# A short convolution before a feed-forward layer: the first convolution in four 64x64 array tiles, a larger first load of w_in, and one x load moved

## The chip, the cores and the metric

The kernel runs on one core of a Trainium2 chip. A core has TensorE (PE in the profile) for matrix products, VectorE (DVE), ScalarE (ACT) and GpSimd (POOL) for elementwise work, SyncE (SP) for issuing transfers, and 16 DMA engines that all queues share. The metric is device time in microseconds. "Before" is the median of five runs.

## The reference

x has 8 batches of 4096 tokens with 192 channels. Eight heads of 24 channels each have seven taps. The taps of a head go through a softmax, and each head convolves its channels causally along the tokens. The result goes through a feed-forward layer with 2048 hidden units and ELU between its two products:

```
w = softmax(weight, axis=-1)                       # 8 heads x 7 taps
att[b, s, h, :] = sum_k w[h, k] * x_pad[b, s + k, h, :]   # six zero rows ahead of s = 0
h = att.reshape(32768, 192) @ w_in                 # 192 x 2048
g = where(h > 0, h, exp(min(h, 0)) - 1)
out = g @ w_out                                    # 2048 x 192
```

The kernel takes and gives FP32, and computes its products in BF16 and FP16 with FP32 accumulation.

## The kernel before

**Tiling.** The 32768 tokens form 32 supergroups of 1024. A supergroup has two groups of 512 tokens, group 0 and 1. Channels are split in three chunks j = 0, 1, 2 of 64 (eight of each head's 24 channels), and chunk data of group 0 lies in partitions 0 to 63, of group 1 in 64 to 127, so one 128-partition tile holds a chunk of both groups. The hidden units are split in 16 blocks q of 128. A step n is one q of one supergroup: for each group r, three H matmuls (L1006, one per chunk, 64 rows by 128 columns of the array, 512 tokens) fill one PSUM bank. One such bank is called a unit here.

**The ELU chain.** Each unit passes ScalarE's exp (L752, H to E), GpSimd's clamp to at most one (L705, on E in place) and VectorE's last step (L868: max(E - 1, H), written to gT in FP16), which also frees the bank. Then the output matmuls (L1029) multiply gT with w_out. The units pass the three engines in one order, each engine in its own program order.

**Order on TensorE.** A planner writes TensorE's order out when the program is built. It has two clocks, one for each group (and row half of the array), and puts H matmuls (h), convolution matmuls (c) and output matmuls (o) where its clocks and its model of the ELU chain say that they can run. The first 16 steps are planned with the function live, the rest by emit. PSUM has eight banks, and a bank that is to be reused waits for its reader. Engines run their lists in order, so an instruction whose wait is open holds everything behind it.

**Start.** Only supergroup 0 is convolved by another path than the rest. x for it arrives in xs. ScalarE casts it to BF16, chunk by chunk (L727, xb). TensorE transposes it (L929) in 64x64 tiles on the array's diagonal, chunk 3 meaning the eight halo rows (L940). VectorE evacuates chunk 0 and the halo (L824) and ScalarE chunks 1 and 2 (L739) to xT, with channels in partitions and tokens along the row. The convolution (L957) is then seven matmuls per chunk, one for each tap, whose 128x128 weights, taps, are diagonal matrices; chunks 0 and 1 leave two taps each to VectorE (L833, L838), which adds them while evacuating (L851). Chunk 2 has all taps on TensorE, in two half rows in two banks, evacuated by ScalarE (L743) and VectorE (L853). The results are att, the input of the first 16 steps. The other supergroups are convolved from xg with a band matrix Tm (L981), which is built in DRAM from wband (VectorE, L816) by two transfers that SyncE issues (L1052, L1061).

**Loads.** GpSimd issues w_in in two sets of three loads (L642: columns of q 0 to 3, then of q 4 to 15), then w_out (L653, three loads) and x of supergroups 1, 2 and 3 (L622, two loads each), and goes to its clamps after that. Later x loads stand between the clamps, at the unit that x_before names. w_in is loaded to partitions 0 to 63; the second copy in partitions 64 to 127, for group 1, is made by ScalarE for q 0 to 3 (L733) ahead of the convolution's last evacuation, by VectorE for q 4 to 7 (L856) after it, by ScalarE for q 8 after the seventh exp, and by a transfer of SyncE (L1069) for q 9 to 15.

The constants that set this:

```
WCOLS = ((0, 4 * FC), (4 * FC, 16 * FC))
UPPER = ((0, 4 * FC), (4 * FC, 8 * FC), (8 * FC, 16 * FC))
X3_AT = (0, 0)
ON_DVE = (2, 2, 0)
```

Of the kernel before, what the change touches and what calls it, by code (L numbers as in the profile page):

```python
# [39 lines left out]
WARM = (6, 1, 4)  # L40
WCOLS = ((0, 4 * FC), (4 * FC, 16 * FC))
UPPER = ((0, 4 * FC), (4 * FC, 8 * FC), (8 * FC, 16 * FC))
WOUT = (0, 4, 8, 16)
X3_AT = (0, 0)
HALO = 8
BW = P
ON_DVE = (2, 2, 0)
XL = GS - CW * (NWIN - 1) + PAD
# [18 lines left out]
ZERO_AT = 8  # L67
TAIL = 18


def bass_lightweight_conv__then__act_elu_kernel(
# [247 lines left out]

    start_up = [("t", j) for j in (0, 3, 1, 2)] + [("d", j) for j in range(3)]  # L320
    for i, (b, what) in enumerate(
# [6 lines left out]
    for rt in range(2):  # L328
        for g in range(2):
            turns[rt][g] += [(0, q, q + 1, 2 * q + rt) for q in range(LIVE - EARLY_O[g])]  # L330
    live(LIVE, [(n, m) for n in range(LIVE) for m in conv_steps.get(n, ())], turns)
    for n in range(LIVE, NP):
# [79 lines left out]
    with ExitStack() as stack:  # L412
# [34 lines left out]
        wcol = sbuf("wcol", [P, KSIZE], FP32)  # L447
        part = sbuf("part", [P, 2, GS], FP32)
        xl = sbuf("xl", [XL, D], FP32)
# [23 lines left out]
        s_xt = sema("s_xt")  # L473
        s_first = sema("s_first")
        s_fa = sema("s_fa")
# [48 lines left out]
        def att_need(s):  # L524
# [8 lines left out]
            ("d", 0): (0, 3),  # L533
            ("d", 1): (0, 4),
            ("d", 2): (3, 5),
        }
# [6 lines left out]
        def transposed(j):  # L543
            if j == 3:
                return xT[:, :, 0:HALO], H[:, bank_of["t", 3], 0 : 3 * HALO].rearrange(
                    "p (j c) -> p j c", j=3
                )
            return xT[:, j, HALO : HALO + GS], H[:, bank_of["t", j], :]

        def first_att(j, c0, c1):  # L550
# [164 lines left out]
        def _scalar(a):  # L715
# [9 lines left out]
            W(s_xs, 16)  # L725
            for j in range(3):
                a.activation(  # L727
                    xb[:, j, :, :].rearrange("p i (h e) -> p (i h) e", e=8),
                    xs[:, :, :].rearrange("p i (h j e) -> p j (i h) e", j=3, e=8)[:, j],
                    ACT.Copy,  # L730
                ).then_inc(s_cast)
            def upper_half(c0, c1):
# [4 lines left out]
            for j in range(1, 3):  # L737
                W(s_xt, j + 2)
                a.activation(*transposed(j), ACT.Copy).then_inc(s_fa)  # L739
            W(s_w[0], 48)  # L740
            upper_half(*UPPER[0])
            W(s_first, 3)
            a.activation(*first_att(2, 0, GS // 2), ACT.Copy).then_inc(s_fa)  # L743
            for item in act_order:
                if item[0] == "c":
                    m = item[1]
                    W(s_cv, m + 1 - CU)
                    a.activation(*conv_evac(W, m), ACT.Copy).then_inc(s_ce)  # L748
                elif item[0] == "h":
                    i = unit_at[item[1:]]  # L750
                    W(s_h, i + 1)
                    a.activation(  # L752
                        E[:, i % NE, :], H[:, bank_of[item], :], ACT.Exp
                    ).then_inc(s_exp)
                    if i == COPY_AT:
                        W(s_w[1], 48)
                        upper_half(UPPER[2][0], FC * LATE_Q)
                else:
                    a.activation(*out_evac(W, *item[1:]), ACT.Copy).then_inc(s_oev[item[2]])  # L759
# [4 lines left out]
        def _vector(v):  # L764
# [3 lines left out]
            v.memset(wband[:], 0.0).then_inc(s_wb)  # L768
            v.memset(xbh[:, :, 0, :], 0.0).then_inc(s_xz)
            W(s_wb, 1)  # L770
# [37 lines left out]
                ALU.mult,  # L808
            ).then_inc(s_tap)
            W(s_xh, 16)  # L810
            W(s_xz, 1)
            v.tensor_copy(
                xbh[:, :, 1, :].rearrange("p j (h e) -> p j h e", e=8),
                xh[:, :].rearrange("p (h j e) -> p j h e", j=3, e=8),
            ).then_inc(s_xz)
            v.tensor_copy(  # L816
# [4 lines left out]
            ).then_inc(s_tap)  # L821
            for at, j in enumerate((0, 3)):
                W(s_xt, at + 1)
                v.tensor_copy(*transposed(j)).then_inc(s_fd)  # L824
            W(s_fd, 2)
            for i in range(ON_DVE[0]):
                for j in range(2):
                    tap = KSIZE - 1 - i
                    src = xT[:, j, HALO - PAD + tap : HALO - PAD + tap + GS]
                    w = wcol[:, tap : tap + 1]  # L830
                    if i == 0:
                        W(s_fa, j)
                        ins = v.tensor_scalar(  # L833
                            out=part[:, j, :], in0=src, scalar1=w, scalar2=None, op0=ALU.mult
                        )
                    else:
                        W(s_part, 2 * i + j - 1)
                        ins = v.scalar_tensor_tensor(  # L838
                            out=part[:, j, :],
                            in0=src,  # L840
                            scalar=w,
                            in1=part[:, j, :],
                            op0=ALU.mult,
                            op1=ALU.add,
                        )
                    ins.then_inc(s_part)
            for j in range(2):
                W(s_part, 2 * ON_DVE[j] - 1 + j)
                W(s_first, j + 1)
                to, at = first_att(j, 0, GS)  # L850
                v.tensor_tensor(to, at, part[:, j, :], ALU.add).then_inc(s_fd)  # L851
            W(s_first, 3)
            v.tensor_copy(*first_att(2, GS // 2, GS)).then_inc(s_fd)  # L853
            c0, c1 = UPPER[1]
            W(s_w[1], 48)
            v.tensor_copy(w_in[HP:P, :, c0:c1], w_in[0:HP, :, c0:c1]).then_inc(s_wc)  # L856
            for item in dve_order:
# [20 lines left out]
        def _tensor(pe):  # L878
            W = Waits(pe)

            def wait_bank(what):
# [9 lines left out]
                else:  # L891
                    evacuated_by(W, *was[1:])

            turns, done = {0: 0, 1: 0}, {}
            for item in pe_order:
# [25 lines left out]
                elif item[0] == "t":  # L921
                    j = item[1]
                    W(s_id, 2)
                    if j < 3:
                        W(s_cast, j + 1)
                        for i in range(XI):
                            for g in range(2):
                                rows = slice(HP * g, HP * (g + 1))
                                ins = pe.matmul(  # L929
                                    H[rows, bank_of[item], i:GS:XI],  # L930
                                    xb[rows, j, i, :],
                                    ident[rows, rows],
                                    start=(i == 0),
                                    stop=(i == XI - 1),
                                    tile_position=(HP * g, HP * g),
                                )
                    else:
                        W(s_xz, 2)
                        for jj in range(3):
# [8 lines left out]
                elif item[0] == "d":  # L948
                    j = item[1]
                    W(s_tap, 3 if j == 2 else 2)  # L950
                    first_evacuated(W, ("t", j))
                    first_evacuated(W, ("t", 3))
                    last = KSIZE - 1 - ON_DVE[j]
                    for tap in range(last + 1):
                        for half in range(2 if j == 2 else 1):
                            c0, c1 = (GS // 2 * half, GS // 2 * (half + 1)) if j == 2 else (0, GS)
                            ins = pe.matmul(  # L957
                                H[:, bank_of[item] + half, c0:c1],
                                taps[:, tap, :],
                                xT[:, j, HALO - PAD + tap + c0 : HALO - PAD + tap + c1],  # L960
                                start=(tap == 0),
                                stop=(tap == last),
                            )
                    ins.then_inc(s_first)
                elif item[0] == "c":
# [27 lines left out]
                elif item[0] == "h":  # L993
                    _, n, r, j = item
                    s, q = divmod(n, NQ)
                    if j == 0:
                        W(s_w[next(k for k in range(2) if FC * q < WCOLS[k][1])], 48)
                        part = next(k for k in range(3) if FC * q < UPPER[k][1])
                        if r == 1:
                            W(*((s_wa, 1), (s_wc, 1), (s_wa, 2))[part] if q < LATE_Q else (s_wd, 16))  # L1000
                        if s:
                            W(s_att[s % 2], att_need(s))
                        wait_bank(item[:3])
# [107 lines left out]
```

## Time and profile before

| | us |
|---|---|
| median of five runs | 719.76 (719.64 to 719.96) |
| profiled execution | 719.64 |
| its span | 717.8 |
| granted TensorE clock | 1.0 of full |

The page divides the span into 40 slices of about 18 us; the first slice of each engine is the least filled one, apart from the last:

```profile
PE   8999999999999999999999999999999999999998
DVE  7999898998898998899998989988989988999994
ACT  6999999999999999999999999999999999999994
```

Each digit is the busy share of one slice in tenths. The costliest groups, with busy time, mean ns of one, and the idle time before them with what ended most of it:

```profile
L868 DVE SCALAR_TENSOR_TENSOR gT<-E,H 128x512 f16<-128x512 f32 x1024 | 631.8, 683 | 62.1 <-POOL E L705 58.2
L1006 PE MATMUL H<-att,w_in 64*128 64x512 bf16 x3072 | 680.1, 376 | 0.8 <-DVE gT L868 0.7
L1029 PE MATMUL H<-w_out,gT 64*128 64x192 f16 x8192 | 680.8, 243 | 0.1
L705 POOL TENSOR_SCALAR E<-E 128x512 f32<-128x512 f32 x1024 | 603.1, 612 | 41.2 <-ACT E L752 34.0
```

The two TensorE rows overlap each other, since matmuls on the two row halves of the array run side by side. Of the transfers, those of w_in land from 5.5 us (the first load) to 12.8 us (the sixth), those of w_out at 14.1, 17.9 and 22.8 us.

### The profile page before, as it was taken

The numbers are of one execution on the slowest core, as the hardware profiler recorded it, in microseconds if no ns is written. First come the engines' busy times: TensorE is split into PE (matmuls) and PEld (weight loads), VectorE is DVE, ScalarE is ACT, GpSimd is POOL, SyncE is SP. The second block draws the span as 40 slices with busy tenths as digits, with TensorE's granted clock in tenths as the row PEclk, the third lists the DMA queues.
The fourth block names the chain that finished last, engine by engine and source line by source line (L and its number), as shares of the span: only waits on it lengthen the run. The fifth ranks groups of instructions, "written<-read, shape, count | busy, mean of one in ns | idle before, by whom it ended". The sixth has DMA issues, their size and how long they took to land.

```text
span 717.8 us, 27609 instructions
## 1 busy us (share of the span) xinstructions
PE 712.2 (99%) x11847; PEld 682.4 (95%) x11847; DVE 641.6 (89%) x1048; ACT 678.4 (95%) x1289; POOL 664.3 (93%) x1112
## 2 busy tenths in 40 slices
PE   8999999999999999999999999999999999999998
PEld 4599999999999999999999999999999999999998
DVE  7999898998898998899998989988989988999994
ACT  6999999999999999999999999999999999999994
POOL 9989999999999999999999999999999999999893
PEclk9999999999999999999999999999999999999999
DMA  9725445554443553454554345554435534435212
GB/s 177 118 60 86 73 74 75 96 86 72 78 84 72 91 94 63 77 86 81 87 89 71 73 75 96 87 70 80 83 74 93 91 62 78 90 77 83 54 52 69
DMA packets 132303, 58.80 MB, mean 82 GB/s; under 512 B 98374, under 2 KB 131604, under 8 KB 132180
## 3 DMA queue, kind: packets, MB, share of 16 engines
q0 software_dynamic: 43504, 16.77, 22.5%
q1 hardware_dynamic: 88388, 39.37, 22.2%
q8 instruction: 93, 1.52, 0.9%
q10 hardware_dynamic: 288, 0.88, 0.4%
q14 instruction: 30, 0.25, 0.1%
HBM read 34.63 MB, written 25.46 MB: 84 GB/s over the span
## 4 chain that ended last, share of the span: by engine, by line
PE 98%; ACT 1%; DVE 0%; POOL 0%; issue 0%; ACTq 0%; DVEq 0%
PE H L1029 55%; PE H L1006 38%; PE H L981 4%; PE H L957 1%; ACT E L752 0%; PE H L929 0%; PE H L903 0%; DVE gT L868 0%; ACT L720 0%; POOL E L705 0%; ACT csb L748 0%; ACTq L717 0%; DVE osb L859 0%; DVE wn L786 0%; ACT scr L720 0%
## 5 line engine op out<-in xcount | busy, mean ns | idle before, releaser
L868 DVE SCALAR_TENSOR_TENSOR gT<-E,H 128x512 f16<-128x512 f32 x1024 | 631.8, 683 | 62.1 <-POOL E L705 58.2
L1006 PE MATMUL H<-att,w_in 64*128 64x512 bf16 x3072 | 680.1, 376 | 0.8 <-DVE gT L868 0.7
L1029 PE MATMUL H<-w_out,gT 64*128 64x192 f16 x8192 | 680.8, 243 | 0.1
L705 POOL TENSOR_SCALAR E<-E 128x512 f32<-128x512 f32 x1024 | 603.1, 612 | 41.2 <-ACT E L752 34.0
L1029 PEld LDWEIGHTS H<-w_out,gT 64*128 64x128 f16 x8192 | 607.4, 94 | 16.9 <-PE H L1029 1.8
L752 ACT ACTIVATE E<-H 128x512 f32<-128x512 f32 x1024 | 585.3, 601 | 23.9 <-PE H L1006 0.8
L1006 PEld LDWEIGHTS H<-att,w_in 64*128 64x128 bf16 x3072 | 274.3, 93 | 7.6 <-issue 1.6
L981 PE MATMUL H<-xg,Tm 64*128 64x240 bf16 x496 | 90.9, 263 | 0.0
L748 ACT ACTIVATE csb<-H 112x480 bf16<-112x480 f32 x124 | 70.9, 572 | 0.1
L759 ACT ACTIVATE osb<-H 128x384 f32<-128x384 f32 (+1 forms) x129 | 61.9, 482 | 6.9 <-PE H L1029 6.8
L622 POOL DMA_DIRECT2D xg<-in_x_dram x62 | 55.3, 902 | 0.2 <-issue 0.2
L981 PEld LDWEIGHTS H<-xg,Tm 64*128 64x128 bf16 x496 | 42.5, 94 | 1.1 <-DVE gT L868 0.3
L859 DVE COPY osb<-H 128x192 f32<-128x192 f32 x1 | 0.4, 358 | 7.3 <-PE H L1029 7.3
L903 PE MATMUL H<-zw 128*128 128x512 bf16 x10 | 4.3, 593 | 1.2 <-DVE zw L767 1.2
L903 PEld LDWEIGHTS H<-zw 128*128 128x128 bf16 x10 | 1.2, 134 | 3.0 <-issue 1.7
L957 PE MATMUL H<-xT,taps 128*128 128x256 bf16 (+1 forms) x24 | 3.9, 317 | 0.0
L727 ACT ACTIVATE xb<-xs 128x512 bf16<-128x512 f32 x3 | 1.7, 619 | 2.2 <-DMA xs<-in_x_dram 2.2
L957 PEld LDWEIGHTS H<-xT,taps 128*128 128x128 bf16 x24 | 2.2, 97 | 1.5
L642 POOL DMA_DIRECT2D w_in<-in_moe_w_in_dram x6 | 3.6, 626 | 0.0
L653 POOL DMA_DIRECT2D w_out<-in_moe_w_out_dram x3 | 2.7, 939 | 0.0
L720 ACT ACT_TABLE_LOAD x1 | 1.3, 1283 | 1.2 <-PEq L1096 1.2
L733 ACT ACTIVATE w_in<-w_in 64x1536 bf16<-64x1536 bf16 (+1 forms) x2 | 2.0, 1002 | 0.0
(43 smaller groups left out, 19.8 us busy)
## 6 DMA issues: line engine op xcount, KB each, us to landing
out_dram<-osb SPq DMA_DIRECT2D x126, 192.0 KB, 2.8
xg<-in_x_dram POOLq DMA_DIRECT2D x61, 240.0 KB, 4.6
xs<-in_x_dram ACTq DMA_DIRECT2D x1, 768.0 KB, 4.4
w_in<-in_moe_w_in_dram POOLq DMA_DIRECT2D x3, 192.0 KB, 5.5
att<-csb SPq DMA_TRANSPOSE x31, 3.9
w_out<-in_moe_w_out_dram POOLq DMA_DIRECT2D x2, 192.0 KB, 8.8
w_out<-in_moe_w_out_dram POOLq DMA_DIRECT2D x1, 384.0 KB, 13.6
w_in<-w_in SPq DMA_DIRECT2D x1, 336.0 KB, 7.1
```

The costliest lines, as they stand in the source:

```text
L622: g.dma_start(xg[0:rows, b, 2 * w0 + gr : 2 * w1 : 2, :], src).then_inc(s_x[b][gr], 16)
L642: g.dma_start(w_in[0:HP, j, c0:c1], bass.AP(tensor=moe_w_in.tensor, offset=8 * j * FF + c0, ap=[[CPH * FF, HEADS], [FF, 8], [1, c1 - c0]], ...
L705: g.tensor_scalar(out=E[:, i % NE, :], in0=E[:, i % NE, :], scalar1=1.0, scalar2=0.0, op0=ALU.min, op1=ALU.max,).then_inc(s_clp)
L748: a.activation(*conv_evac(W, m), ACT.Copy).then_inc(s_ce)
L752: a.activation(E[:, i % NE, :], H[:, bank_of[item], :], ACT.Exp).then_inc(s_exp)
L759: a.activation(*out_evac(W, *item[1:]), ACT.Copy).then_inc(s_oev[item[2]])
L868: v.scalar_tensor_tensor(out=gT[:, s % NG3, q, u, :], in0=E[:, i % NE, :], scalar=1.0, in1=H[:, bank_of[item], :], op0=ALU.subtract, op1=A ...
L903: pe.matmul(H[:, bank, :], zw[:, 0:P], zw[:, 0:GS], start=True, stop=True)
L957: ins = pe.matmul(H[:, bank_of[item] + half, c0:c1], taps[:, tap, :], xT[:, j, HALO - PAD + tap + c0 : HALO - PAD + tap + c1], start=(tap ...
L981: ins = pe.matmul(H[:, bank_of["c", m], 256 * q : 256 * q + UC], Tm[rows, h, :], xg[rows, s % NXB, :, CPH * h : CPH * (h + 1)].rearrange(" ...
L1006: ins = pe.matmul(H[:, bank_of[item[:3]], :], w_in[HP * r : HP * (r + 1), j, FC * q : FC * (q + 1)], att[HP * r : HP * (r + 1), s % 2, j, ...
L1029: ins = pe.matmul(acc_of(k, g)[:, D * kb : D * (kb + 1)], gT[HP * rt : HP * (rt + 1), t % NG3, q, g, t0 : t0 + P], w_out[HP * rt : HP * (r ...
```

## The change

The first convolution uses the array as four tiles of 64x64. The diagonal weights need no full array: the 64 channels of a group in one chunk only meet their own weights. Chunk 1's two groups are exchanged on the way: its transpose writes group 0 to partitions 64 to 127 and group 1 to 0 to 63, and its convolution exchanges them back, so that chunk 1 uses the two tiles off the diagonal while chunks 0 and 2 use those on it. The matmuls of two lists (chunk 0 then chunk 2; chunk 1) are interleaved by their columns. VectorE takes three taps of chunk 0 and none of chunk 1. ScalarE evacuates all of chunk 1, and VectorE makes chunk 1's cast of x. The halo copy is split, because chunk 1's halo is exchanged too, and the halo is transposed after chunk 1 rather than after chunk 0.

w_in comes in two equal sets, q 0 to 7 and q 8 to 15. Its upper copy is made for q 0 and q 1 by ScalarE, each by itself, after the convolution's last evacuation, and for q 2 to 3 and 4 to 7 by VectorE. The planner's clock of row group 1 starts 600 ns late, so that group 0 comes first in the first steps. The load of group 1 of x of supergroup 3 moves from before the first clamp to before the clamp of unit 48.

```diff
-WCOLS = ((0, 4 * FC), (4 * FC, 16 * FC))
-UPPER = ((0, 4 * FC), (4 * FC, 8 * FC), (8 * FC, 16 * FC))
+WCOLS = ((0, 8 * FC), (8 * FC, 16 * FC))
+UPPER = ((0, FC), (FC, 2 * FC), (2 * FC, 4 * FC), (4 * FC, 8 * FC), (8 * FC, 16 * FC))
-X3_AT = (0, 0)
+X3_AT = (0, 48)
-ON_DVE = (2, 2, 0)
+ON_DVE = 3
+UPPER_LATE = 600.0
...
-    start_up = [("t", j) for j in (0, 3, 1, 2)] + [("d", j) for j in range(3)]
+    start_up = [("t", j) for j in (0, 1, 3, 2)] + [("d",)]
...
+    clock[1] = UPPER_LATE
     live(LIVE, [(n, m) for n in range(LIVE) for m in conv_steps.get(n, ())], turns)
...
             W(s_xs, 16)
-            for j in range(3):
-                a.activation(
...
+            for j in (0, 2):
+                a.activation(*cast(j), ACT.Copy).then_inc(s_cast)
...
             for j in range(1, 3):
-                W(s_xt, j + 2)
+                W(s_xt, 2 * j)
                 a.activation(*transposed(j), ACT.Copy).then_inc(s_fa)
+            W(s_first[1], 1)
+            a.activation(*first_att(1, 0, GS), ACT.Copy).then_inc(s_fa)
+            W(s_first[2], 1)
+            a.activation(*first_att(2, 0, GS // 2), ACT.Copy).then_inc(s_fa)
             W(s_w[0], 48)
-            upper_half(*UPPER[0])
-            W(s_first, 3)
-            a.activation(*first_att(2, 0, GS // 2), ACT.Copy).then_inc(s_fa)
+            for k in range(2):
+                upper_half(*UPPER[k])
...
+            W(s_xs, 16)
+            v.tensor_copy(*cast(1)).then_inc(s_castv)
             W(s_xh, 16)
             W(s_xz, 1)
...
-            for at, j in enumerate((0, 3)):
-                W(s_xt, at + 1)
+            for at, j in ((1, 0), (3, 3)):
+                W(s_xt, at)
                 v.tensor_copy(*transposed(j)).then_inc(s_fd)
             W(s_fd, 2)
-            for i in range(ON_DVE[0]):
-                for j in range(2):
...
+            for i in range(ON_DVE):
+                tap = KSIZE - 1 - i
+                src = xT[:, 0, HALO - PAD + tap : HALO - PAD + tap + GS]
...
+            W(s_part, ON_DVE)
+            W(s_first[0], 1)
+            to, at = first_att(0, 0, GS)
+            v.tensor_tensor(to, at, part[:], ALU.add).then_inc(s_fd)
+            W(s_first[3], 1)
             v.tensor_copy(*first_att(2, GS // 2, GS)).then_inc(s_fd)
-            c0, c1 = UPPER[1]
-            W(s_w[1], 48)
-            v.tensor_copy(w_in[HP:P, :, c0:c1], w_in[0:HP, :, c0:c1]).then_inc(s_wc)
+            W(s_w[0], 48)
+            for c0, c1 in UPPER[2:4]:
+                v.tensor_copy(w_in[HP:P, :, c0:c1], w_in[0:HP, :, c0:c1]).then_inc(s_wc)
...
                 elif item[0] == "d":
...
+                    rows_of = [
+                        [(0, tap, 0, GS, 0) for tap in range(KSIZE - ON_DVE)]
+                        + [(2, t, GS // 2 * c, GS // 2 * (c + 1), 2 + c) for c in range(2) for t in range(KSIZE)],
+                        [(1, tap, 0, GS, 1) for tap in range(KSIZE)],
+                    ]
+                    merged, ends = [], [0, 0]
+                    while any(rows_of):
+                        d = min((d for d in range(2) if rows_of[d]), key=lambda d: ends[d])
+                        piece = rows_of[d].pop(0)
+                        ends[d] += piece[3] - piece[2]
+                        merged.append(piece)
...
+                        for r in range(2):
+                            rows, to = half_of(r), half_of(r ^ (j == 1))
                             ins = pe.matmul(
-                                H[:, bank_of[item] + half, c0:c1],
-                                taps[:, tap, :],
-                                xT[:, j, HALO - PAD + tap + c0 : HALO - PAD + tap + c1],
+                                H[to, bank_of["d", j] + (j == 2 and c0 > 0), c0:c1],
+                                taps[rows, tap, rows],
+                                xT[rows, j, HALO - PAD + tap + c0 : HALO - PAD + tap + c1],
                                 start=(tap == 0),
                                 stop=(tap == last),
+                                tile_position=(rows.start, to.start),
                             )
```

## The prediction

> **What bounds the kernel now.** I read the page's rows by engine and its costliest groups first, then the writers of gT counted by stretch, then the first 16 us as a timeline. Five runs have a median of 719.76 us; the profiled one took 719.64, its span is 717.8, so 1.84 us lie around the span. A change of the span is carried to the median one for one.
>
> ```profile
> PE 712.2 (99%) x11847; PEld 682.4 (95%) x11847; DVE 641.6 (89%) x1048; ACT 678.4 (95%) x1289; POOL 664.3 (93%) x1112
> ```
>
> The share says TensorE, but it is an average over stages. The table below counts L868, the last step of the ELU, which frees a PSUM bank and makes gT; columns are busy us and, in brackets, the instructions touching the stretch.
>
> ```profile
> 14.30:24.60 10.30, 10.26 (x17) 1.00 1.50 219
> 24.60:28.90 4.30, 3.70 (x6) 1.00 0.66 97
> 28.90:37.90 9.00, 9.00 (x16) 1.00 0.15 30
> 59.70:81.50 21.80, 19.75 (x33) 1.00 0.45 80
> 668.40:689.70 21.30, 20.00 (x33) 1.00 0.28 60
> ```
>
> From 14.3 to about 38 us VectorE is saturated (0.60 us a unit, 17 units in 10.3 us), but for a dent at 24.6 to 28.9, where 6 units take 4.3 us instead of 3.6: waits for ScalarE. From then on the pace is TensorE's, about 0.66 to 0.68 us a unit, to the end. TensorE has slack before 38 us, so whatever moves the first L868 moves the whole kernel, if no transfer is late. What the first L868 (14.32) waits for is in the timeline:
>
> ```profile
> 5.24 1.67 ACT L727 ACTIVATE xb<-xs 128x512 bf16<-128x512 f32 x3 [2.19 <-DMA xs<-in_x_dram]
> 6.60 0.78 DVE L824 CAST xT<-H 128x512 bf16<-128x512 f32 x2 [0.51 <-PE H L929]
> 6.64 1.08 PE L929 MATMUL H<-ident,xb 64*64 64x64 bf16 x32
> 7.66 3.88 PE L957 MATMUL H<-xT,taps 128*128 128x512 bf16 x24
> 10.05 3.58 POOL L622 DMA_DIRECT2D xg<-in_x_dram  x4
> 11.57 0.38 ACT L743 ACTIVATE att<-H 128x256 bf16<-128x256 f32 x1 [1.66 <-PE H L957]
> 12.56 3.54 ACT L752 ACTIVATE E<-H 128x512 f32<-128x512 f32 x7 [0.60 <-PE H L1006]
> 12.80 0.69 DVE L856 COPY w_in<-w_in 64x1536 bf16<-64x1536 bf16 x1 [0.80 <-DMA w_in<-in_moe_w_in_dram]
> 13.66 2.92 POOL L705 TENSOR_SCALAR E<-E 128x512 f32<-128x512 f32 x5
> ```
>
> The first exp (L752) starts at 12.56 and is done at 13.16. GpSimd's clamp L705 starts only at 13.66, because GpSimd issues its fourth x load until 13.63. So two chains end here, and the later is GpSimd's list of loads, by 0.5 us.
>
> **The change, part by part.**
>
> *Four-tile convolution.* Before: 10 matmuls of 512 columns and 14 of 256, that is 17 streams of 512. The row gives 3.88 less a last tail of 0.27, 3.61 / 17 = 0.212 us each. After: two interleaved lists, chunk 0 with 4 taps of 512 and then chunk 2 with 14 pieces of 256 (11 streams of 512), chunk 1 with 7 of 512; each piece is two 64x64 matmuls. If the four tiles run together the longer list counts: 11 x 0.212 = 2.33 us, 1.28 less. It starts when VectorE has evacuated chunk 0 and the halo (7.38 now) and the last transposes are issued. I put the start at 7.5, since the halo's evacuation stays behind chunk 0's on VectorE; 7.66 now. Chunk 1's list may wait until 7.65 for ScalarE, it has slack. The end is 7.5 + 2.33 + tail 0.27 + 0.1 = 10.2 against 11.54.
>
> *What the faster convolution waits for next.* VectorE does three taps of chunk 0 instead of two each of chunks 0 and 1. From 7.42: one L833 (0.55 or 0.86 measured) + two L838 (0.73) + the addition L851 (0.68) with about 0.03 between dependent ones: 10.2 to 10.5. Then the cast of half of chunk 2 (0.42): 10.65 to 10.9. ScalarE evacuates all of chunk 1 (0.6) from 9.4 and its half of chunk 2 (0.38) by 10.3. The first H group then ends at about 11.2, and exp starts near 11.3 against 12.56: 1.3 us earlier.
>
> *Casts.* One of ScalarE's three casts (0.61) goes to VectorE, nearest row L812 (192 elements in 0.27) scaled to 512: 0.6. It and the split halo copy (two for one, +0.15) lie ahead of wband L816; overlapping as VectorE does, wband is 0.5 us later, so the band's write is issued at 6.6 and not 6.12. It holds no transpose of chunk 0. The band and Tm return chain (7.0 + 5.6 us) ends at 18.75 now; first use is at 20.5. After: 19.2 against a use at 19.0 to 19.6. Cost 0 to 0.3, taken 0.
>
> *w_in.* Six issues before and after. Set 0 has 384 KB in bf16 instead of 192. Before, the first 192 KB landed at 6.73 and 192 more at 8.95; so s_w[0] is at about 9, over 1 us ahead of its first user. ScalarE's copy of 1.48 us, hidden under the convolution, becomes two of 0.52 (the existing 64x384 L733) between the evacuations and exp 0: done by 10.7 and 11.15, just when H group 0 ends. VectorE copies 768 and 1536 elements, 0.35 + 0.69, before 12, in a hole that ends with the first L868. Without the hole they would cost their 1.04 us. TensorE starts with row group 0 and takes group 1 some 0.6 us later, the time of the first upper copy.
>
> *x load of supergroup 3, group 1.* Its issue goes from the start to unit 48. GpSimd's loads end one step of 0.85 earlier (four in 3.58, the last 1.03 long), so the first clamp is at 12.8. Since exp 0 ends at 11.9, GpSimd remains the late one: **the start gains 0.85 us, not 1.3**. At unit 48 (about 43 us, TensorE's pace) the issue of 0.9 us delays clamps, later recovered at 0.58 a unit. The price is bounded by 0 and 0.9; nearest row: stretches with two such loads take 21.8 us for the same 33 instructions, the one without takes 21.3, and lacks one convolution unit (four 240-column matmuls on two row groups, 0.2): 0.15 a load. I take 0.2. It lands some 5 us after issue, its convolution comes about 12 units (8 us) later.
>
> *Order.* Row group first, two banks exchanged, the first output products three H matmuls earlier; the two orders are the same from step 16 on, up to a permutation of banks. Bounds -0.5 and +0.5, taken 0.
>
> **Two rules against rows.** (1) The Trainium skill, "DMA: Bandwidth & Descriptors", section SWDGE vs HWDGE vs iDMA, says VectorE in its two-port mode locks GpSimd out of the SBUF into which it writes descriptors. VectorE's copies would then stop the load list for 1.04 us, the first clamp would be at 13.8, and the gain -0.2. The row: L856 (0.69) lies inside the fourth x issue (12.59 to 13.63), which took 1.035 us against 1.00 for its neighbours; it cost 0.03. By the row the loss is 0.05, which I neglect. (2) "TensorEngine Tiling (Array Packing)", Gotcha 1, says row tiles can't access one PSUM bank at the same time. Chunk 0's two tiles do, in different partition halves. The nearest row, L929, also writes two 64x64 tiles to one bank: 32 in 1.08 us, (1.08 - 0.24) / 15 = 0.056 a pair. But 64 columns stream in 0.027, so a pair one after the other would fit as well; the trace doesn't decide it. By the rule, with the two chunks still side by side: (8 x 0.212 + 28 x 0.106) = 4.7 us, ending at 12.5; by full overlap 10.2. I take overlap, because the halves share no partition.
>
> **Sum.** 717.8 - 0.85 + 0.2 = 717.15 for the span; median 719.76 - 0.65 = **719.1 us**.
>
> **Rivals.**
> A. *The dent closes too.* ScalarE will be 0.45 us further ahead of GpSimd than now; the dent (4.3 instead of 3.6 us at 24.6, and a smaller one, 0.86 in all) is VectorE waiting for exps. If the new order and the lead close it: -0.85 - 0.86 + 0.2 = -1.5, 718.3. For it: those units wait for ScalarE. Against: the loop of five or six banks sets that wait, and these do not become more.
> B. *The tiles exclude each other* (slower). All 50 matmuls one after another: 22 x 0.212 + 28 x 0.106 = 7.6 us, end at 15.4, exp 0 at 16.4, its clamp at 17.1 instead of 13.66: +3.4 + 0.2, 723.4. With only same-bank tiles exclusive, end 12.5, clamp 14.3: +0.8, 720.6. It gives a slower kernel beyond noise once the convolution takes over about 5.7 us. For it: rule 2. Against: the main loop's paired row groups do run together, and different column groups should.
> C. *A transfer takes the gain.* The later band, or a slot lost behind the saturated queue (DMA share 1.5 to 1.6 at 14 to 17 us), holds TensorE 0.5 to 1 us at the first convolution unit: 719.6 to 720.1. That the gain is hidden anyway is the same time.
>
> **Chances.** Forecast 0.43 (its own range 718.4 to 719.6), A 0.34, B 0.15, C 0.08. A measurement of this kernel tells about 0.2%, 1.44 us, from no change: faster is under 718.3, slower over 721.2. Forecast and C are within; A is at or past the edge (its late part 0.02 within), B mostly slower, with its milder form within, and some unnamed loss from the new order is slower: faster 0.34, same 0.48, slower 0.18. The 0.02 of A's late part is made up by the forecast's early tail. The range for 8 in 10 is 717.9 to 721.0.
>
> **What the changed profile would show.** Four-tile matmuls ending near 10.2 with pieces every 0.21 us (B: 12.5 or later); exp 0 near 11.3; three L622 before the first clamp, which starts at 12.8; first gT near 13.45 and 17 units at 0.6; a lone x issue near 43 us followed by a short slip; no wait for the band at the first 64x240 matmul. A first clamp after 13.5, or a gain at 38 us that is gone at 60, would make the prediction wrong.

## The result, and the profile after

| | before | after |
|---|---|---|
| median, us | 720.14 (719.64 to 721.47, 41 runs) | 718.63 (718.33 to 718.82, 21 runs) |
| profiled execution, us | 719.64 | 718.54 |
| its span, us | 717.8 | 716.6 |
| first convolution's matmuls, us from the start | 7.66 to 11.54 | 7.62 to 10.21 |
| first exp | 12.56 | 11.29 |
| end of GpSimd's first loads | 13.63 | 12.70 |
| first writer of gT | 14.32 | 13.39 |

The ratio of the times is 0.9978 (95% interval 0.9972 to 0.9984): 1.5 us or 0.22% less. Over 41 runs beside the changed kernel, the median of before is 720.14 rather than the 719.76 of the first five. So a part of the 1.5 us can't be seen in the two profiles: the profiled execution of before was its fastest, and the two spans differ by 1.2.

The rows by engine, VectorE's slices and two of the costliest groups of the changed kernel (the ELU's last step is L871 now, the H matmuls L1029, the output matmuls L1052, the clamp L714, the exp L760):

```profile
PE 710.5 (99%) x11873; PEld 681.5 (95%) x11873; DVE 642.4 (90%) x1049; ACT 677.5 (95%) x1290; POOL 663.4 (93%) x1112
...
DVE  8999889998898998899998999988989988999994
...
L871 DVE SCALAR_TENSOR_TENSOR gT<-E,H 128x512 f16<-128x512 f32 x1024 | 632.2, 683 | 61.8 <-POOL E L714 57.6
...
L714 POOL TENSOR_SCALAR E<-E 128x512 f32<-128x512 f32 x1024 | 603.0, 612 | 41.2 <-ACT E L760 34.3
```

Almost nothing moves here: the four costliest groups are the same within 0.5 us, and VectorE's first slice goes from 7 to 8. A change worth 0.2% is not seen in totals. It is seen in the start, and in how far the rest keeps what the start gained. The timeline of the start, from 7 us (start, length, and in brackets the engine's idle time before and what ended it):

```profile
6.85 0.37 SPq L1075 DMA_DIRECT2D conv_band<-wband  x1
...
7.62 2.59 PE L978 MATMUL H<-xT,taps 64*64 64x512 bf16 x50
...
10.05 2.65 POOL L631 DMA_DIRECT2D xg<-in_x_dram  x3
...
10.71 1.65 DVE L859 COPY w_in<-w_in 64x768 bf16<-64x768 bf16 x2
...
11.29 2.56 ACT L760 ACTIVATE E<-H 128x512 f32<-128x512 f32 x5
12.63 1.30 POOL L714 TENSOR_SCALAR E<-E 128x512 f32<-128x512 f32 x2
...
13.39 0.69 DVE L871 SCALAR_TENSOR_TENSOR gT<-E,H 128x512 f16<-128x512 f32 x1 [1.03 <-POOL E L714]
```

The convolution ends 1.33 us earlier and exp 0 starts 1.27 earlier; exp 0 is done at 11.9. The clamp starts only at 12.63, when GpSimd has issued three x loads instead of four. The first gT is 0.93 earlier. The writers of gT in the stretches shown of before (columns as there: stretch, its length, VectorE's busy time with the instructions, clock, DMA):

```profile
14.30:24.60 10.30, 10.26 (x18) 1.00 1.41 210
24.60:28.90 4.30, 3.92 (x7) 1.00 0.59 92
...
59.70:81.50 21.80, 19.78 (x33) 1.00 0.44 79
668.40:689.70 21.30, 20.03 (x33) 1.00 0.28 60
```

The pace is the same as before, and the dent at 24.6 us is still there, a little filled (3.92 us of busy time instead of 3.70). To see where the 0.93 us goes, the start of each unit's writer of gT is compared between the two traces. Minus means earlier than before:

| unit | after less before, us | what happened since the row above |
|---|---|---|
| 0 to 13 | -0.93 | the start |
| 19 to 47 | -1.07 | units 14 to 21, the dent: -0.14 |
| 48 | -0.28 | the moved load: +0.79 at once |
| from 53 | -0.67 | half of that is caught up: +0.40 in all |
| 1023 (last) | -0.93 | -0.26, in eight steps of 0.03, seven of them 128 units (one batch) apart |
| end of the span | -1.21 | -0.28 in the last stores, which vary from one execution to another |

The stores' share: from the start of the last gT to the end of the span it takes 10.6 to 11.0 us in the twelve traces of the changed kernel and of its variants below, 11.1 in before and 12.0 in experiment 1, the other trace with the old start. One of SyncE's last store issues takes 1.24 us in before and 2.06 in experiment 1. Two traces are too few to tell whether this is chance or belongs to the old kernel.

### The profile page after: what moved, and what is told of

The parts are those of the page before. It is cut to its first block, busy times and chain, and to the rows that moved or that the text cites. A ratio compares the mean times of both kernels' runs of the same rounds, so it can differ in the third digit from the quotient of the medians.

```text
span 716.6 us, 27662 instructions
## 1 busy us (share of the span) xinstructions
PE 710.5 (99%) x11873; PEld 681.5 (95%) x11873; DVE 642.4 (90%) x1049; ACT 677.5 (95%) x1290; POOL 663.4 (93%) x1112
## 4 chain that ended last, share of the span: by engine, by line
PE 96%; POOL 2%; ACT 1%; DVE 0%; issue 0%; DVEq 0%; POOLq 0%
PE H L1052 54%; PE H L1029 37%; PE H L1004 4%; POOL xg L631 1%; ACT E L760 1%; POOL E L714 1%; POOL w_in L651 0%; POOL w_out L662 0%; DVE gT L871 0%; ACT csb L756 0%; POOL owner L679 0%; DVE osb L862 0%; POOL block L689 0%; POOL ident L668 0%; POOL ones L666 0%
## 5 line engine op out<-in xcount | busy, mean ns | idle before, releaser
L871 DVE SCALAR_TENSOR_TENSOR gT<-E,H 128x512 f16<-128x512 f32 x1024 | 632.2, 683 | 61.8 <-POOL E L714 57.6
L1029 PE MATMUL H<-att,w_in 64*128 64x512 bf16 x3072 | 679.9, 376 | 1.2 <-DVE gT L871 0.9
L1052 PE MATMUL H<-w_out,gT 64*128 64x192 f16 x8192 | 680.5, 243 | 0.1
L714 POOL TENSOR_SCALAR E<-E 128x512 f32<-128x512 f32 x1024 | 603.0, 612 | 41.2 <-ACT E L760 34.3
L1052 PEld LDWEIGHTS H<-w_out,gT 64*128 64x128 f16 x8192 | 606.4, 94 | 17.6 <-PE H L1052 1.5
L760 ACT ACTIVATE E<-H 128x512 f32<-128x512 f32 x1024 | 585.0, 600 | 23.8 <-PE H L1029 0.4
L1029 PEld LDWEIGHTS H<-att,w_in 64*128 64x128 bf16 x3072 | 275.2, 93 | 7.8 <-DVE gT L871 3.1
L1004 PE MATMUL H<-xg,Tm 64*128 64x240 bf16 x496 | 90.9, 263 | 0.0
L1004 PEld LDWEIGHTS H<-xg,Tm 64*128 64x128 bf16 x496 | 42.7, 94 | 1.2 <-DVE gT L871 0.3
L909 PE MATMUL H<-zw 128*128 128x512 bf16 x10 | 4.1, 563 | 1.2 <-DVE zw L775 1.2
L909 PEld LDWEIGHTS H<-zw 128*128 128x128 bf16 x10 | 1.1, 128 | 2.9 <-issue 1.6
L978 PE MATMUL H<-xT,taps 64*64 64x256 bf16 (+1 forms) x50 | 2.6, 317 | 0.0
L978 PEld LDWEIGHTS H<-xT,taps 64*64 64x64 bf16 x50 | 2.0, 105 | 0.4
```

The costliest lines, as they stand in the source:

```text
L714: g.tensor_scalar(out=E[:, i % NE, :], in0=E[:, i % NE, :], scalar1=1.0, scalar2=0.0, op0=ALU.min, op1=ALU.max,).then_inc(s_clp)
L760: a.activation(E[:, i % NE, :], H[:, bank_of[item], :], ACT.Exp).then_inc(s_exp)
L871: v.scalar_tensor_tensor(out=gT[:, s % NG3, q, u, :], in0=E[:, i % NE, :], scalar=1.0, in1=H[:, bank_of[item], :], op0=ALU.subtract, op1=A ...
L909: pe.matmul(H[:, bank, :], zw[:, 0:P], zw[:, 0:GS], start=True, stop=True)
L978: ins = pe.matmul(H[to, bank_of["d", j] + (j == 2 and c0 > 0), c0:c1], taps[rows, tap, rows], xT[rows, j, HALO - PAD + tap + c0 : HALO - P ...
L1004: ins = pe.matmul(H[:, bank_of["c", m], 256 * q : 256 * q + UC], Tm[rows, h, :], xg[rows, s % NXB, :, CPH * h : CPH * (h + 1)].rearrange(" ...
```

## The experiments

The theory after the result: the start ends with the later of two chains, exp 0 and GpSimd's list of loads, and both have to be shorter. The rival: the shorter convolution makes the gain by itself, and the load is a side matter. In what follows "gain" is the first gT's, against before, if nothing else is said. "Level" is the start of a unit's writer of gT less that of before, as in the table above. All ratios are to before, on the same chip.

**1. The load alone.** Before, with one constant changed:

```diff
-X3_AT = (0, 0)
+X3_AT = (0, 48)
```

> The kernel before with only the second x load of supergroup 3 moved to unit 48. Theory 1 (the start is set by the later of GpSimd's list of loads and the first exp): the list ends at 12.7, but exp 0 still ends at 13.15, so the first clamp starts at 13.2 and the first gT at 13.85, 0.45 us earlier than before; the moved load then costs 0.4 at unit 48, and the span stays within 0.2 us of 717.8. Theory 2 (the shorter convolution makes the gain by itself): the start doesn't move, and the moved load costs nothing or 0.4: span 717.8 to 718.2, first gT at 14.3.

Measured: 720.49, ratio 0.9999 (0.9991 to 1.0008). Its timeline:

```profile
10.04 2.71 POOL L622 DMA_DIRECT2D xg<-in_x_dram  x3
...
12.64 2.56 ACT L752 ACTIVATE E<-H 128x512 f32<-128x512 f32 x5 [0.60 <-PE H L1006]
13.33 1.76 POOL L705 TENSOR_SCALAR E<-E 128x512 f32<-128x512 f32 x3 [0.58 <-ACT E L752]
...
13.98 1.29 DVE L868 SCALAR_TENSOR_TENSOR gT<-E,H 128x512 f16<-128x512 f32 x2 [0.70 <-POOL E L705]
```

GpSimd is free at 12.75 and now waits 0.58 us for exp 0: the first gT comes 0.34 earlier and no more, since the old convolution is the late chain. At unit 48 the load's price takes that away (the level is +0.05 from unit 53 on).

**2. All but the load.** The changed kernel with `X3_AT = (0, 0)`:

> The changed kernel with that load put back before the first clamp. Theory 1: convolution and exp 0 stay early (exp 0 at 11.3), but the first clamp waits for the list of loads until 13.5 and the first gT starts at about 14.2, only 0.1 us earlier than before; nothing is paid at unit 48; span 717.2 to 717.6, a gain of at most a third. Theory 2: the start keeps its gain of about 0.9 and the price at unit 48 goes, so the span is 716.2.

Measured: 719.66, ratio 0.9994 (0.9985 to 1.0003). Its timeline:

```profile
7.72 0.37 SPq L1075 DMA_DIRECT2D conv_band<-wband  x1
...
10.05 3.50 POOL L631 DMA_DIRECT2D xg<-in_x_dram  x4
...
12.04 3.53 ACT L760 ACTIVATE E<-H 128x512 f32<-128x512 f32 x7
13.48 1.88 POOL L714 TENSOR_SCALAR E<-E 128x512 f32<-128x512 f32 x3
14.24 1.28 DVE L871 SCALAR_TENSOR_TENSOR gT<-E,H 128x512 f16<-128x512 f32 x2 [1.03 <-POOL E L714]
...
20.59 0.27 PE L1004 MATMUL H<-xg,Tm 64*128 64x240 bf16 x1 [0.51 <-DMA Tm<-conv_band]
```

The convolution is four-tiled, exp 0 is done 0.8 us before the clamp starts, and the first gT is only 0.08 earlier. The start gains 0.34 by one part and 0.08 by the other, and 0.93 by both together. That is the mark of two chains of which the later one counts, and the rival falls.

The time of this run is a weaker witness than its first gT, since it holds another cost, the prediction's case C. In the profiled execution the convolution's weights came late, so the band was issued at 7.72 instead of 6.85, Tm landed at 20.5, and TensorE stood 0.51 us for it (the level is +0.51 from unit 19 on). Five of the eleven executions, with a mean granted clock of 0.995 to 0.998, took 720.4 to 721.7 us; the six at 1.0 took 718.9 to 719.7. What lowered the clock in the five was not traced; experiment 4 shows one way.

**3. Without the exchange.** The changed kernel, with all chunks on the diagonal tiles (three places; the halo's slot goes with it):

```diff
-                                rows, to = half_of(g), half_of(g ^ (j == 1))
+                                rows, to = half_of(g), half_of(g)
...
-                            rows, to = half_of(r), half_of(r ^ (j == 1))
+                            rows, to = half_of(r), half_of(r)
```

> The changed kernel with chunk 1's groups not exchanged, so all pieces use the two diagonal tiles. Theory 1: the two lists then share tiles and follow each other, 11 + 7 - 7 streams of the first four tiles become 4 + 7 + 7 = 18 of 512 columns for TensorE: 3.8 us instead of 2.3 to 2.5, ending at 11.5; exp 0 at about 12.5, the first clamp at 13.15 and the first gT at 13.85, span about 717.0. Rival: the array runs the pieces together anyhow, or the exchange is only needed for something else: convolution 2.5 us, first gT at 13.4, span 716.6 as with the change.

Measured: 719.64, ratio 0.9992 (0.9983 to 1.0).

```profile
7.96 4.11 PE L978 MATMUL H<-xT,taps 64*64 64x512 bf16 x50
...
13.09 2.06 ACT L760 ACTIVATE E<-H 128x512 f32<-128x512 f32 x4
...
13.79 1.19 POOL L714 TENSOR_SCALAR E<-E 128x512 f32<-128x512 f32 x2 [0.83 <-ACT E L760]
...
14.43 0.69 DVE L871 SCALAR_TENSOR_TENSOR gT<-E,H 128x512 f16<-128x512 f32 x1 [0.63 <-POOL E L714]
```

The same 50 matmuls take 4.11 us instead of 2.59: 18 streams of 512 columns at 0.212 us and a tail, so the two chunks follow each other on the diagonal, and a pair on one bank still runs together. Exp 0 is the late chain again. (The convolution began 0.34 us later than in the changed kernel, x being late, so the first gT's 14.43 is not all due to the edit.) The exchange is what makes the convolution four tiles wide.

**4. The load later.** The changed kernel with `X3_AT = (0, 53)`:

> The changed kernel with the moved load at unit 53 instead of 48. In the kernel before, GpSimd waited some 0.4 us for an exp ahead of unit 53 and hardly at all ahead of unit 48. Theory 1: the first gT stays at 13.4 and the delay of gT at the load shrinks from 0.8 to about 0.5, and what is lost for good from 0.4 to about 0.2: span 716.3 to 716.4. Rival: the price of a load doesn't depend on its place, or x comes too late for its convolution at unit 60: span 716.6 or more.

Measured: 722.79, ratio 1.0031 (1.0018 to 1.0044), slower than before. This was a miss. GpSimd, then TensorE, then TensorE's busy time by stretch (with granted clock, DMA share and GB/s):

```profile
45.65 0.89 POOL L631 DMA_DIRECT2D xg<-in_x_dram  x1
46.56 4.06 POOL L714 TENSOR_SCALAR E<-E 128x512 f32<-128x512 f32 x7
53.76 0.61 POOL L714 TENSOR_SCALAR E<-E 128x512 f32<-128x512 f32 x1 [3.13 <-ACT E L760]
```
```profile
52.43 0.36 PE L1004 MATMUL H<-xg,Tm 64*128 64x240 bf16 x1 [2.83 <-issue]
```
```profile
49.60:52.40 2.80, 0.00 (x0) 1.00 1.28 165
52.45:55.87 3.42, 3.42 (x32) 0.50 0.03 5
55.87:60.00 4.13, 4.13 (x74) 1.00 0.14 48
```

The load was issued at 45.65 and landed 6.7 us later, at 52.3. TensorE's next convolution matmul (L1004, from xg) starts at 52.43 after 2.83 us of nothing; the view names no releaser ("issue"), but the landing is just ahead of it. The clamps then have nothing to do for 3.13 us. TensorE stood from 49.6: with the 4.6 us that the changed kernel's page gives as the median landing, the load would have come at 50.25 and been late too. The deadline for its issue is between unit 48, where nothing waited, and unit 53.

The standing is not the whole price. The level goes from -0.78 to +3.69, by 4.47 us, of which TensorE stood 2.83. When it went on, its granted clock was 0.50 for 3.4 us, which costs half of that, 1.7 us; the two make 4.5. The times agree: the three executions with a mean granted clock of 1.0 took 720.8 to 721.3 us, the seven with 0.995 to 0.998 took 722.5 to 724.8.

**5. The order alone undone.** The changed kernel with `UPPER_LATE = 0.0`:

> The changed kernel with the planner's clock of row group 1 not set back (0 instead of 600), so that TensorE's order and the banks are those of before. Theory 1 (the order adds only the 0.15 us that gT gains between units 14 and 21): first gT at 13.4 as with the change, 0.93 ahead at unit 22 instead of 1.07; span 716.7, within 0.2 of the change. Rival: the order is what lets exp 0 start at 11.3, since group 1 must wait for ScalarE's copy: exp 0 at 11.6 or later, but the first clamp still at 12.6; then also 716.7 and the order is hidden. Rival 2: the order makes part of the later slow gain of 0.26 us between units 60 and 1000: then that is absent and the span is 717.0.

Measured: 718.8, ratio 0.9979 (0.997 to 0.9987). Exp 0 is at 11.91, 0.6 later (0.2 of it because the convolution began later), and hidden behind GpSimd: the first gT gains 0.73, its 0.2 less coming from GpSimd's issues, two of which took longer, so that its list ends at 12.90 instead of 12.70. The level stays within 0.02 of that to unit 47, so the 0.14 in the dent belongs to the order. The slow gain after unit 53 is there here too, so the order is not its cause.

**6 and 7. Both loads of supergroup 3 moved.** `X3_AT = (37, 45)`, and `(17, 45)`:

> The changed kernel with both x loads of supergroup 3 between the clamps, at units 37 and 45, ahead of which GpSimd waited 0.2 to 0.3 us for exps. Theory 1: the list of loads ends at 11.9, as exp 0 does (11.9), so the first clamp starts at 11.95 and the first gT at 12.6, 1.7 us ahead of before; the two loads cost 0.3 to 0.6 together; span 716.0 to 716.3. Rival: VectorE's copies of w_in, which end at 12.4, collide with the first clamps and hold gT back to 13.0 or later, or the order around units 14 to 21 can't use the earlier start: span 716.5 or more.

> As e6, with the loads at units 17 and 45. In the dent at units 17, 19 and 21 GpSimd waits 0.9 us in all for exps, so a load at 17 is hidden if those waits are fixed in time: span 715.9. If the waits come from the loop of banks (a late gT makes the next exps late too), the load costs its 0.5 to 0.9 there, as VectorE sets the pace: span 716.3 to 716.7.

Measured: 718.52, ratio 0.9973 (0.9962 to 0.9983), and 718.84, ratio 0.9979 (0.997 to 0.9988). The first gT gains 1.47 and 1.61: with two loads fewer GpSimd is done at 12.10 and 11.99, when exp 0 is done too (12.04 and 11.98), so the two chains are level. From unit 53 on 0.86 is left of the 1.47: the loads cost 0.45 and 0.10 for good at their places. In the other kernel much of the 1.61 goes before its load is reached: TensorE comes to the first convolution from xg before Tm has landed.

```profile
19.07 0.27 PE L1004 MATMUL H<-xg,Tm 64*128 64x240 bf16 x1 [0.53 <-DMA Tm<-conv_band]
```

The band was not late here (issued at 6.86, Tm landed at 19.03). At unit 14 this takes 0.81 of the 1.61, and the loads at 17 and 45 take the rest: -0.80 becomes -0.30 by unit 21 and -0.14 from unit 53 on. With both loads moved, the start's gain above 0.93 is thus paid back in part at the loads' new places and, in the second kernel, in part to Tm. In these two kernels there is no slow gain.

**8. The load three units earlier.** `X3_AT = (0, 45)`, run twice, the second time beside the change itself:

> The changed kernel with the moved load at unit 45 instead of 48. GpSimd waits 0.3 us ahead of unit 45, and again 0.4 ahead of unit 53. Theory 1: gT is 0.5 us late at 45 instead of 0.8 at 48, and what is left for good after unit 53 is 0.1 to 0.2 instead of 0.4: span 716.3. Rival: what is left for good doesn't depend on the place (0.4): span 716.6.

> The kernel of e8 again, beside the changed kernel on the same chip. Theory 1: 0.2 to 0.3 us faster than the changed kernel. Rival: the same within 0.1.

> The changed kernel unaltered, as the partner of the other three: ratio 0.998 to before, first gT at 13.4 to 13.65, span 716.4 to 716.8 by how long GpSimd's loads take to issue in that execution.

Measured: 718.42 (0.9974, 0.9963 to 0.9984); again 718.5 (0.9972, 0.9961 to 0.9983) beside the change's 718.68 (0.9972, 0.9962 to 0.9983). In the traces the load's price for good is 0.14 and 0.13 at unit 45, and 0.40 at unit 48 in both traces of the change. The times differ by 0.2 us in the same direction with intervals that overlap: a better place by the trace, not shown by the times.

**9. w_in's sets as before.** The changed kernel with q 0 to 3 as set 0 again, VectorE's second copy waiting for set 1:

```diff
-WCOLS = ((0, 8 * FC), (8 * FC, 16 * FC))
+WCOLS = ((0, 4 * FC), (4 * FC, 16 * FC))
...
             for c0, c1 in UPPER[2:4]:
+                W(s_w[c0 // (4 * FC)], 48)
```

> The changed kernel with the first w_in set holding q 0 to 3 again, so that VectorE's copy for q 4 to 7 waits for the second set. Theory 1: the second set lands at 12.8, so that copy (0.7 to 1.2) runs from 12.8 to 13.5 or 14.0, beside GpSimd's first clamps and ahead of the first gT, which starts at 13.5 to 14.1 instead of 13.4: span 716.7 to 717.2. Rival: VectorE's hole takes it and nothing changes: first gT at 13.4, span 716.6.

Measured: 719.73, ratio 0.9999 (0.9982 to 1.0017), 1.05 us over the change on the same chip (718.68), though the two intervals just touch. So the edit of w_in is probably needed, by more than expected, and how the 1.05 comes about stays open. The profiled execution began late, with late weights as in experiment 2 (the convolution at 8.90, Tm landed at 20.2). In it VectorE's second copy, the cost that was expected, ran from 12.88 to 13.55 and held nothing, the first gT being at 14.13; against a first gT at 13.39 a copy that ends there would cost 0.16.

**10. ScalarE half a microsecond later.** The changed kernel with one more copy of w_in, of 0.5 us, to a buffer that nobody reads, ahead of ScalarE's two:

```diff
+            c0, c1 = UPPER[0]
+            a.activation(spare[HP:P, :, :], w_in[0:HP, :, c0:c1], ACT.Copy)
```

> The changed kernel with one more copy on ScalarE (0.43 to 0.52 us, to a buffer that nobody reads) ahead of its two copies of w_in, so that exp 0 ends 0.5 later, at 12.35. Theory 1: GpSimd's list ends at 12.6 to 12.7, so the first clamp and the first gT stay where they are within 0.05 us (12.65 and 13.4), and the span at 716.6 within 0.2: 0.5 us of what the convolution gained is not used. Theory 2 (exp 0 sets the start): all is 0.5 later, span 717.1.

Measured: 718.65, ratio 0.9972 (0.9961 to 0.9982), against 718.68 for the change on the same chip. Half a microsecond more on exp 0's chain costs nothing in the times, as it should be when GpSimd's list is 0.7 later. Its trace can't be read for the start, since x came late in that execution.

The parts that make the new convolution (the moved cast and taps, the evacuations, the copies on ScalarE) were not undone one by one; only the exchange was.

## Why the prediction was right or wrong

The time is in the predicted range and the sign was right, but the gain was forecast at 0.65 us or 0.09%, and is 1.5 us or 0.22% (0.16 to 0.28%). Over half of it came from terms that the sum had at 0 or not at all. That the time still lies in the range is owed to the range's width, and is partly luck. Rival A's time (718.3) was nearer than the forecast, though not by rival A's mechanism.

- **The two chains: right.** Exp 0 was put near 11.3 and is at 11.29; the clamp at 12.8 and is at 12.63; the first gT at 13.45 and is at 13.39. The forecast used only 0.85 of the 1.27 us; experiments 2 and 10 show that the rest is unused. It gave 0.93, since the three x issues were 0.08 shorter than taken.
- **The four-tile convolution: right.** It took 2.59 us, against 2.33 and a tail of 0.27, in rounds of four matmuls every 0.215 us. The choice against Gotcha 1 of the Trainium skill's "TensorEngine Tiling (Array Packing)" was right for this case: two row tiles that write one bank, in separate partition halves, ran at full rate, so B fell. Experiment 3 is the rate with two tiles.
- **Casts and band: the cost right, by a faster transfer.** The band was issued at 6.85 (6.6 forecast), but Tm landed at 18.57 (19.2 forecast, 18.75 before), as the chain took 11.7 us instead of 12.6. Its first use was at 19.00, so 0.4 us of the 1.8 before is left. Experiments 2 and 7 show C's mechanism, with a band 0.9 us later and with a start 0.7 us earlier than the change's.
- **VectorE's copies beside the load list: right in time, wrong in who pays.** The rule of the Trainium skill's "DMA: Bandwidth & Descriptors" (SWDGE vs HWDGE vs iDMA) would have made GpSimd later, to a start 0.2 us behind that of before. The three issues took 0.94 to 0.96, not more than before. But VectorE's second copy took 1.19 us, where the same size took 0.69 before, and 0.67 in the traces of experiments 9 and 10 and in the second trace of the change (taken with experiment 8), where no issue ran beside it. In experiments 5, 7 and the second run of 8 the copy took 0.67 beside an issue, and that issue took 1.01 to 1.04, some 0.13 more than its neighbours. In 6 and the first run of 8 the copy took 1.19 and every x issue 1.08 or more, but there the issues were long before the copies began. So running side by side cost VectorE 0.5 us or GpSimd 0.13. On VectorE it is hidden, because its next gT is at 13.39 and the copy ends at 12.36.
- **The moved load's price: the mechanism right, the size off.** Forecast 0.2, from a row of two loads in the steady pace; measured 0.40, made up of the two steps in these lines of GpSimd in the changed kernel:

```profile
41.43 1.19 POOL L714 TENSOR_SCALAR E<-E 128x512 f32<-128x512 f32 x2
42.56 0.89 POOL L631 DMA_DIRECT2D xg<-in_x_dram  x1
43.48 2.91 POOL L714 TENSOR_SCALAR E<-E 128x512 f32<-128x512 f32 x5
```

  The issue fills 0.89 us between two clamps, the next clamps follow each other at 0.58, and what they don't catch up stays. Three units earlier the same issue costs 0.14. The price is a matter of the place, not of the engine's average slack. The prediction let the use come 8 us after the issue; from the issue at 42.56 to where TensorE stood in experiment 4, at 49.6, it is 7, and five units later (3.1 us) the issue missed it.
- **Order: taken 0, measured -0.14** (the dent, which experiment 5 gives back). Rival A had put 0.86 there and most of the dent stayed. That fits the argument against A, a loop of five or six banks, which was not tested by itself.
- **Not in the sum at all: -0.26 and -0.28.** The slow gain was not foreseen, and neither was the earlier landing of the last stores. The first appears in the kernels in which exactly one load was moved, and not in before or in experiments 2, 6 and 7. In the former an x issue between clamps takes 882 ns as the median, in the latter 894. Unit by unit, the level falls by 0.015 to 0.02 at each x issue (units 101 and 109, then every 32 units); the 0.03 of two issues is mostly given back eight units later, and is kept at the eight steps. Why the issues are shorter was not tested, and stays open. The second varies between executions, as said above.

The failed step is the sum: the start is 0.08 more, the load costs 0.20 more, and three terms put at 0 were -0.14, -0.26 and -0.28. That makes -1.21 instead of -0.65 for the span, and the two profiled executions differ by 1.10. The other 0.4 of the measured 1.5 is that before's profiled execution, the base of the sum, was 0.5 faster than its median of 41 runs and the changed kernel's only 0.1. Experiments show the causes of the start's 0.93, of the load's price and of the order's 0.14; those of the slow gain, of the stores and of this 0.4 are open.

## What to carry to other kernels

Where two chains end close together, a cut of one is worth only the distance to the other, so two edits can pay more together than the sum of what each pays alone (0.93 against 0.34 and 0.08 here): test each alone and both, before one is dropped. An issue moved off a crowded start is paid at its new place, less what the engines there can catch up, and it has a deadline, which is when its data is wanted less a landing time that varies. Missing it can cost more than the wait, if TensorE stands long enough to lose its clock. For a gain of 0.2%, compare the two traces unit by unit: each row of such a table is one term of the sum.

## What the runs showed of the hardware that was not expected

**A wait of 2.8 us halved TensorE's clock.** In experiment 4 TensorE stood for 2.83 us, and the granted clock was then 0.50 until 55.87. The Trainium skill, "TensorE: Matmul & The Clock Gate" (What's actually happening), gives half rate as the default state and as the state after an idle window of about 3.4 us, and full rate after about 3.4 us of sustained work; here less than that idle time was enough, and the half rate lasted 3.4 us.

**The start varies by over 1 us between executions of one kernel,** by when x arrives and by when TensorE comes to its full rate. In the second profile of the changed kernel, taken with experiment 8, x was in use only at 6.01 us instead of 5.34, and TensorE stood 0.43 us before its transposes:

```profile
6.69 1.46 PE L936 MATMUL H<-ident,xb 64*64 64x64 bf16 x32 [0.43 <-ACT xb L736]
...
9.07 3.13 PE L978 MATMUL H<-xT,taps 64*64 64x512 bf16 x48
...
13.23 2.06 ACT L760 ACTIVATE E<-H 128x512 f32<-128x512 f32 x4
```

By the starts of its matmuls, the rounds of four then came every 0.43 us until 10.2 us and every 0.22 after that, so the convolution took 3.36 us instead of 2.59, exp 0 was the late chain, and the first gT came at 14.57. In experiment 10's profile, with a gap of 0.89 us from 6.26 to 7.15, the same change of rate was at 10.4. The half rate was not brought on by these gaps. In both traces TensorE's first matmuls, on zeros and with no result that is used (L909), already came every 0.43 us from 1.6 us to the gap; in the changed kernel's first trace the last two, from 5.1 on, are 0.22 us apart. A gap as long did no harm to an array already at full rate, in the second run of experiment 8:

```profile
6.24 0.86 PE L936 MATMUL H<-ident,xb 64*64 64x64 bf16 x32 [0.85 <-ACT xb L736]
```

Its matmuls on zeros came every 0.22 us ahead of the gap, and its convolution took the 2.59 us of the changed kernel's. Whether a gap at the half rate puts the full rate off was not tested.

**Landing varies.** Loads of this size landed 4.6 us after issue as the median of the changed kernel; the moved load alone landed after 3.9 to 6.7 us in twelve traces, 6.7 in experiment 4.
